# A linear-attention and gated-MLP kernel: the two x tiles move from the end of every partition to a place ahead of the weights

## The chip, the cores and the metric

The kernel runs on one core of a Trainium2 chip. The metric is the time of one execution on the device in microseconds (us); lower is better. Several executions are timed and their median is given, and one further execution is recorded by the hardware profiler; all rows below come from that one.

## The reference

A recurrence over 768 steps (batch 4, 8 heads of 48 channels) gives y, and y, laid out as 3072 tokens of 384 channels, goes through a gated two-layer network.

```python
for t in range(S):
    kt, vt, rt = (k[:, :, t], v[:, :, t], r[:, :, t])
    cur = np.einsum('bhd,bhe->bhde', u[None] * kt, vt)
    y[:, :, t] = np.einsum('bhd,bhde->bhe', rt, state + cur)
    state = w[None, :, :, None] * state + np.einsum('bhd,bhe->bhde', kt, vt)
...
x = np.ascontiguousarray(y.transpose(0, 2, 1, 3)).reshape(B * S, H * D)
gate = 1.0 / (1.0 + np.exp(-(x @ w_gate)))
val = x @ w_val
return (gate * val @ w_out).astype(np.float32)
```

The decays w are drawn between 0.85 and 0.95.

## The kernel before, in words

**Tiling.** Time is cut into 12 chunks of 64 steps; two chunks make one x tile of 512 columns (64 steps by 4 batches, twice), so there are six x tiles, `xt[0]` to `xt[5]`. Each is `[128, 4, 2, 512]` in four-byte numbers, 16,384 bytes in every partition: the second index is a group of channels, the third tells the rounded value from its rest. Products are made in three passes (rest of weights by rounded x, rounded by rounded, rounded weights by rest of x), so that they come near full precision.

**Recurrence.** For each of 24 groups (chunk, half of the heads) the kernel loads `chan` (r and k by channel) and `toks` (k and v by token), makes scores, applies them, and adds the state's part; `x_high` (L465, ScalarE) writes the rounded result from PSUM into the x tile, `x_low` (L469, VectorE) the rest, and `fills` (L473, DMA) moves the fourth group's rows into the free rows of the other three.

**Network.** For each x tile and each of 12 slices f of the hidden dimension, `up` (L506) makes two outputs with 9 matmuls of 512 columns each, one PSUM bank after the other; `sigmoid` (L515), `product` (L519), `h_high` (L524) and `h_low` (L528) make the tile `h`; `down` (L544) adds 9 matmuls to three accumulators in three banks, in turn; for the last slice of a tile, `down` goes through the accumulators one after the other instead. Weights come once from memory, are joined from two words, split into rounded value and rest, and stay in SBUF as `wx`, 12 tiles.

**Order.** The order of the instructions on every engine is fixed: a list of steps written out by hand (`START`) up to slice 11 of the first x tile, then a loop over the other five tiles, in which `SLOTS` says after which slices a group of the recurrence is done. All DMAs go through SyncE's queue.

**Places in SBUF.** Pools are laid out one behind the other in the order in which they are opened: the constants (`const`, up to byte 33,792 of each partition, with what lies ahead of it), the weights (`wp`, 33,792 to 144,384), `hp` with the tile `sg` (to 148,480), `hq` with `h` (to 156,672), `wtmp` with `wf` (to 165,888), then `ach` with three `chan` (to 178,176), `atk` with three `toks` (to 187,776), `adk` with two `dec` (to 195,968) and `xp` with the two slots of the x tiles, 195,968 to 212,352 and 212,352 to 228,736. Even x tiles lie in the first slot, odd ones in the second. In `const` lie among others `score` (from 18,112) and `state` (from 22,208).

**General path.** `ach`, `atk`, `adk` and `xp` belong to `main`, which is closed at the end (L695). Then every engine reads a flag and branches (L696, L697): only if a decay is outside 0.5 to 2 is the whole work done again by a slower path, whose tiles take the place that `main` gave up. With these inputs that path isn't entered.

Of the kernel before, what the change touches and what calls it, by code (L numbers as in the profile page):

```python
# [10 lines left out]
F32 = mybir.dt.float32  # L11
F32R = mybir.dt.float32r
# [8 lines left out]
P = 128  # L21
# [4 lines left out]
CT = B * C  # L26
# [33 lines left out]
def rwkv_then_moe(ctx: ExitStack, tc: tile.TileContext, wd, ub, ch, tk, rt, wt, rk0, vn0, wd0, out):  # L60
    nc = tc.nc

    const = ctx.enter_context(tc.tile_pool(name="const", bufs=1))
    wp = ctx.enter_context(tc.tile_pool(name="wp", bufs=1))
    hp = ctx.enter_context(tc.tile_pool(name="hp", bufs=2))
    hq = ctx.enter_context(tc.tile_pool(name="hq", bufs=2))
# [4 lines left out]
    main = ctx.enter_context(ExitStack())  # L71
    ach = main.enter_context(tc.tile_pool(name="ach", bufs=3))
    atk = main.enter_context(tc.tile_pool(name="atk", bufs=3))
    adk = main.enter_context(tc.tile_pool(name="adk", bufs=2))
    xp = main.enter_context(tc.tile_pool(name="xp", bufs=2))


    def two_banks():
# [173 lines left out]
    xt, dec, ga, yb = {}, {}, {}, {}  # L252
# [297 lines left out]
    def accumulators():  # L550
        return [pacc.tile([P, 512], F32, name=f"acc{d}") for d in range(3)]

    def store(acc, dst):
        for d in range(3):
            if d < 2:
                wide = wtmp.tile([P, W3], F32, name="wf")
            o = wide[:, 512 * (d // 2) : 512 * (d // 2) + 512]
            nc.scalar.copy(out=o[:, 0:CT], in_=acc[d][:, 0:CT])
            nc.vector.tensor_copy(o[:, CT:], acc[d][:, CT:])
            nc.sync.dma_start(  # L560
                out=out[d * P : (d + 1) * P, dst], in_=o.rearrange("q (c t) -> q c t", t=CT)
            )
# [70 lines left out]
    for step in START.split():  # L633
        name, _, arg = step.partition(".")
# [62 lines left out]
    with tc.If(bad != 0):  # L697
        with ExitStack() as g:
            gp = g.enter_context(tc.tile_pool(name="gp", bufs=1))
# [21 lines left out]
            with tc.For_i(0, NC) as c:  # L721
# [38 lines left out]
                    out=xg[bass.ds(c, 1)].rearrange("o q p t -> (o q) p t"),  # L760
                    in_=yc.rearrange("q p b i -> q p (b i)"),
                )
            xr = gp.tile([P, 3, 2, CT], F32, name="xr")
            x = gp.tile([P, 3, 2, 512], F32R, name="xgr")
            with tc.For_i(0, NC, 2) as c:
                for j in range(3):
                    for to, lo, n, p in (
                        (0, 0, D, j), (64, 64, D, j), (D, 16 * j, 16, 3), (64 + D, 64 + 16 * j, 16, 3),
                    ):
                        nc.sync.dma_start(  # L770
                            out=xr[to : to + n, j],
                            in_=xg[bass.ds(c, 2), lo : lo + n, p].rearrange("c q t -> q c t"),
                        )
                xf = xr.rearrange("q j c t -> q j (c t)")
                nc.vector.tensor_copy(x[:, :, 0], xf)
                nc.vector.tensor_tensor(x[:, :, 1], xf, x[:, :, 0], ALU.subtract)
                m = Moe(x, accumulators(), slice(0, 512))
                for f in range(NF):
                    m.up(f)
                    m.gate(f)  # L780
                    if f:
                        m.down(f - 1)
                m.down(NF - 1)
                store(m.acc, bass.ds(c, 2))
# [90 lines left out]
```

## Time and profile before

| | |
|---|---|
| median of 3 runs | 558.22 us (557.37 to 559.66) |
| the profiled execution's own time | 559.26 us |
| its span, first to last instruction | 557.5 us |
| TensorE matmuls busy | 521.9 us (94% of the span) |
| VectorE, ScalarE, GpSimd busy | 235.4, 184.1, 212.9 us |
| DMA | 47.84 MB, mean 86 GB/s |
| instructions in the profile | 11987 |

The own time is longer than the span by 1.8 us, which lie before the first and behind the last instruction. Busy times of several engines overlap; a matmul's duration reaches into the next one's, so that its pace is read from the starts of consecutive groups.

### The profile page before, as it was taken

How to read it: one execution, taken by the hardware profiler on the slowest of the kernel's cores; microseconds unless marked ns; L12 is line 12 of the kernel's file. 1: busy time of each engine (PE TensorE's matmuls, PEld its weight loads, DVE VectorE, ACT ScalarE, POOL GpSimd, SP SyncE). 2: the span in 40 equal slices, each digit the busy share in tenths (PEclk: the TensorE clock that was granted, in tenths of full speed). 3: DMA queues.
4: the chain of work that ended last, by engine and by line, in shares of the span. 5: the costliest groups of instructions: out<-in, count | busy, mean ns of one | idle time of the engine just before them, and what ended most of it. 6: DMA issues, size and time to landing. Idle time of an engine off the chain costs nothing. (4 is left out here: it accounts for less than half of the span.)

```text
span 557.5 us, 11987 instructions
## 1 busy us (share of the span) xinstructions
PE 521.9 (94%) x5204; PEld 427.1 (77%) x5204; DVE 235.4 (42%) x364; ACT 184.1 (33%) x394; POOL 212.9 (38%) x165
## 2 busy tenths in 40 slices
PE   1596899999999999999999999999999999999994
PEld 1486778777888888888888888888888888888883
DVE  7798799786524414324414324314324110101001
ACT  4466454633422322422322422322322221221111
POOL 3534234648254424254424254424234121111220
PEclk9998799999999999999999999999999999999998
DMA  8698911040221303221303221303220001100001
GB/s 329 265 364 311 368 36 54 30 111 2 88 83 52 92 16 86 79 77 67 92 15 88 77 80 65 93 13 89 78 75 5 11 1 19 58 0 1 0 1 61
DMA packets 15723, 47.84 MB, mean 86 GB/s; under 512 B 2384, under 2 KB 5200, under 8 KB 14256
## 3 DMA queue, kind: packets, MB, share of 16 engines
q1 hardware_dynamic: 15664, 47.01, 24.7%
q8 instruction: 43, 0.70, 0.5%
q14 instruction: 16, 0.13, 0.1%
HBM read 39.92 MB, written 4.72 MB: 80 GB/s over the span
## 5 line engine op out<-in xcount | busy, mean ns | idle before, releaser
L506 PE MATMUL ring<-xt,wx 128*128 128x512 f32 (+1 forms) x1332 | 317.8, 392 | 1.2 <-PE sc L366 0.8
L506 PEld LDWEIGHTS ring<-xt,wx 128*128 128x128 f32 x1332 | 248.2, 191 | 57.7 <-PE sc L366 0.9
L528 POOL TENSOR_TENSOR h<-sg,h 128x512 fp32r<-128x512 f32 x68 | 97.6, 1435 | 272.4 <-ACT h L524 272.4
L544 PE MATMUL acc<-h,wx 128*128 128x512 f32 (+1 forms) x666 | 164.6, 391 | 2.6 <-DVE h L528 1.3
L519 DVE TENSOR_TENSOR sg<-ring,sg 128x512 f32<-128x512 f32 (+1 forms) x74 | 50.0, 676 | 247.0 <-PE ring L506 247.0
L544 PEld LDWEIGHTS acc<-h,wx 128*128 128x128 f32 x666 | 122.4, 190 | 29.6 <-DVE h L528 1.5
L515 ACT ACTIVATE sg<-ring 128x512 f32<-128x512 f32 (+1 forms) x74 | 43.3, 586 | 158.9 <-PE ring L506 158.9
L524 ACT CAST h<-sg 128x512 fp32r<-128x512 f32 (+1 forms) x74 | 45.0, 608 | 150.6 <-DVE sg L519 150.6
L284 POOL TENSOR_TENSOR dec<-chan,tabk 128x512 f32<-128x512 f32 x22 | 30.7, 1397 | 12.4 <-ACT xt L465 6.9
L469 DVE TENSOR_TENSOR xt<-ring,xt 112x256 fp32r<-112x256 f32 (+1 forms) x52 | 20.0, 419 | 34.6 <-ACT xt L465 32.9
L249 POOL TENSOR_TENSOR wx<-wf,wx 128x1152 fp32r<-128x1152 f32 (+1 forms) x9 | 23.7, 2639 | 24.1 <-ACT wx L246 24.1
L295 DVE TENSOR_TENSOR chan<-chan,tabk 128x512 f32<-128x512 f32 x24 | 28.8, 1201 | 2.9 <-ACT dec L278 2.9
L366 PE MATMUL sc<-dec,chan 48*64 48x64 f32 x768 | 17.9, 236 | 12.2 <-DVE chan L295 10.2
L305 POOL TENSOR_TENSOR dec<-dec,toks 128x384 f32<-128x384 f32 x16 | 16.8, 1050 | 24.6 <-DMA dec<-in_rt 24.5
L366 PEld LDWEIGHTS sc<-dec,chan 48*64 48x64 f32 x768 | 15.3, 148 | 13.6 <-DVE chan L295 9.4
L299 POOL TENSOR_TENSOR toks<-toks,tabn 128x384 f32<-128x384 f32 x19 | 25.4, 1342 | 0.0
L374 DVE COPY_PREDICATED score<-masks,sc 128x512 f32<-128x512 int32 x32 | 23.9, 746 | 0.7
L328 PE MATMUL ring<-score,toks 64*48 64x64 f32 (+1 forms) x768 | 17.0, 226 | 7.5 <-DVE score L374 6.5
L419 ACT ACTIVATE state<-state,pw 112x96 f32<-112x96 f32 x80 | 23.4, 364 | 0.3 <-PE ring L328 0.2
L328 PEld LDWEIGHTS ring<-score,toks 64*48 64x48 f32 (+1 forms) x768 | 14.5, 134 | 8.6 <-issue 7.4
L240 DVE SCALAR_TENSOR_TENSOR wf<-wr,wf 128x1152 int32<-128x1152 int32 (+1 forms) x13 | 20.2, 1552 | 0.4
L239 DVE SCALAR_TENSOR_TENSOR wf<-wr,wf 128x1152 int32<-128x1152 int32 (+1 forms) x13 | 19.8, 1523 | 0.5
(61 smaller groups left out, 275.2 us busy)
## 6 DMA issues: line engine op xcount, KB each, us to landing
wr<-in_wt SPq DMA_DIRECT2D x11, 1152.0 KB, 11.9
chan<-in_ch SPq DMA_DIRECT2D x24, 512.0 KB, 4.0
toks<-in_tk SPq DMA_DIRECT2D x24, 400.0 KB, 4.4
out_y<-wf SPq DMA_DIRECT2D x17, 256.0 KB, 2.3
dec<-in_rt SPq DMA_DIRECT2D x16, 192.0 KB, 2.7
xt<-xt SPq DMA_DIRECT2D x30, 64.0 KB, 2.3
wr<-in_wt SPq DMA_DIRECT2D x2, 576.0 KB, 5.3
xt<-xt SPq DMA_DIRECT2D x12, 32.0 KB, 3.6
```

The costliest lines, as they stand in the source:

```text
L284: eng.tensor_tensor(v4(t[:, 0]), v4(chan[n][:, 0]), bc2(table_of(n)[:, :, ::-1]), ALU.mult)
L295: nc.vector.tensor_tensor(v4(k), v4(k), bc2(table_of(n)), ALU.mult)
L299: eng.tensor_tensor(v4(k), v4(k), bc2(tabn[:, 4 * g : 4 * g + 4]), ALU.mult)
L328: nc.tensor.matmul(yb[n][bank][64 * half : 64 * half + m, cs], lhsT, rhs, start=first, stop=stop, skip_group_check=True,)
L366: nc.tensor.matmul(sc[64 * gm : 64 * gm + 64, be, o : o + C], kk[row, cs : cs + C], rr[row, cs : cs + C], start=True, stop=True,)
L374: nc.vector.copy_predicated(t.rearrange("q (b m i) -> q b m i", b=2, m=4), masks[:, m].bitcast(I32).unsqueeze(1).unsqueeze(1).broadcast_to ...
L506: nc.tensor.matmul(o[:, self.cols], w[a][:, g * DM + kt * P : g * DM + (kt + 1) * P], self.x[:, kt, b, self.cols], start=(k == 0), stop=(k ...
L515: nc.scalar.activation(sg[:, c], self.pair[f][0][:, c], AF.Sigmoid)
L519: nc.vector.tensor_tensor(sg[:, c], self.pair.pop(f)[1][:, c], sg[:, c], ALU.mult)
L524: nc.scalar.copy(out=h[:, 0, c], in_=sg[:, c])
L528: eng.tensor_tensor(h[:, 1, c], self.sg.pop(f)[:, c], h[:, 0, c], ALU.subtract)
L544: nc.tensor.matmul(self.acc[d][:, self.cols], w[a][:, 2 * DM + d * P : 2 * DM + (d + 1) * P], h[:, b, self.cols], start=(f == 0 and k == 0 ...
```

## The change

The pool of the x tiles, `xp`, is opened right behind `const` and no longer as the last of `main`. With that the x tiles lie at bytes 33,792 to 66,560, and every pool from `wp` to `adk` lies 32,768 bytes higher: the weights at 66,560 to 177,152, `h` at 181,248 to 189,440, `wf` to 198,656, `chan` to 210,944, `toks` to 220,544, `dec` to 228,736. As `main` now gives up less room, the general path takes its two large tiles, `xr` and `x`, from `xp`.

```diff
@@ -61,6 +61,7 @@
     const = ctx.enter_context(tc.tile_pool(name="const", bufs=1))
+    xp = ctx.enter_context(tc.tile_pool(name="xp", bufs=2))
     wp = ctx.enter_context(tc.tile_pool(name="wp", bufs=1))
...
     adk = main.enter_context(tc.tile_pool(name="adk", bufs=2))
-    xp = main.enter_context(tc.tile_pool(name="xp", bufs=2))
...
-            xr = gp.tile([P, 3, 2, CT], F32, name="xr")
-            x = gp.tile([P, 3, 2, 512], F32R, name="xgr")
+            wide = xp.tile([P, 4, 2, 512], F32, name="xt")
+            xr = wide[:, 0:3, 0].rearrange("q j (c t) -> q j c t", t=CT)
+            x = xp.tile([P, 4, 2, 512], F32R, name="xt")[:, 0:3]
...
-                xf = xr.rearrange("q j c t -> q j (c t)")
+                xf = wide[:, 0:3, 0]
```

## Rows read from the trace of the kernel before

**Rows 1.** Stretches: busy us (count) of PE, PEld, DVE, ACT, POOL; clock, DMA, GB/s.

```profile
0.00:150.00 150.00, 121.70 (x1789) 102.37 (x1790) 123.17 (x163) 75.21 (x155) 71.38 (x53) 0.97 0.48 175
150.00:548.00 398.00, 398.00 (x3410) 323.49 (x3408) 111.16 (x199) 107.90 (x238) 140.98 (x112) 1.00 0.17 52
```

**Rows 2.** TensorE's longest waits, 0 to 150 us: total, times, longest.

```profile
PE sc L366 <- DVE chan L295: 10.2, 2, 9.4
PE ring L328 <- DVE score L374: 6.5, 2, 6.1
```

**Rows 3.** Timeline of TensorE, a slice of xt[4]: start, us, count.

```profile
440.20 4.36 PE L506 MATMUL ring<-xt,wx 128*128 128x512 f32 x18
444.39 2.22 PE L544 MATMUL acc<-h,wx 128*128 128x512 f32 x9
446.45 0.86 PE L506 MATMUL ring<-xt,wx 128*128 128x512 f32 x3
```

**Rows 4.** Timeline of TensorE, a slice of xt[5].

```profile
491.45 4.35 PE L506 MATMUL ring<-xt,wx 128*128 128x512 f32 x18
495.64 2.22 PE L544 MATMUL acc<-h,wx 128*128 128x512 f32 x9
497.70 4.36 PE L506 MATMUL ring<-xt,wx 128*128 128x512 f32 x18
```

**Rows 5.** Timeline of TensorE, a slice of xt[1].

```profile
210.29 4.34 PE L506 MATMUL ring<-xt,wx 128*128 128x512 f32 x18
214.47 2.25 PE L544 MATMUL acc<-h,wx 128*128 128x512 f32 x9
216.56 4.35 PE L506 MATMUL ring<-xt,wx 128*128 128x512 f32 x18
```

**Rows 6.** The last down: matmuls running at 549.2 and 550.5 us; its weight loads.

```profile
548.99 0.39 PE L544 MATMUL acc<-h,wx 128*128 128x512 f32 x1
...
550.15 0.39 PE L544 MATMUL acc<-h,wx 128*128 128x512 f32 x1
...
548.65 1.46 PEld L544 LDWEIGHTS acc<-h,wx 128*128 128x128 f32 x7 [0.78 <-POOLq L697]
```

**Rows 7.** Groups of the whole span: count, busy us, mean ns, idle before.

```profile
L519 DVE TENSOR_TENSOR sg<-ring,sg 128x256 f32<-128x256 f32 x4 | 1.7, 419 | 3.0 <-PE ring L506 3.0
L469 DVE TENSOR_TENSOR xt<-ring,xt 112x256 fp32r<-112x256 f32 x44 | 16.6, 419 | 32.3 <-ACT xt L465 32.3
L465 ACT CAST xt<-ring 112x256 fp32r<-112x256 f32 x44 | 13.8, 364 | 6.4 <-PE ring L328 6.4
L558 ACT COPY wf<-acc 128x256 f32<-128x256 f32 x15 | 5.5, 373 | 2.5 <-PE acc L544 2.4
```

**Rows 8.** Groups from 150 to 548 us: small matmuls and weight loads.

```profile
L328 PE MATMUL ring<-dec,state 48*64 48x64 f32 x240 | 10.2, 224 | 0.0
L328 PE MATMUL ring<-score,toks 64*64 64x64 f32 x240 | 9.5, 218 | 0.0
L328 PEld LDWEIGHTS ring<-score,toks 64*64 64x64 f32 x240 | 8.2, 135 | 0.0
L328 PEld LDWEIGHTS ring<-dec,state 48*64 48x64 f32 x240 | 8.2, 134 | 5.6 <-issue 5.6
```

**Rows 9.** GpSimd's groups from 150 to 548 us.

```profile
L528 POOL TENSOR_TENSOR h<-sg,h 128x512 fp32r<-128x512 f32 x59 | 80.9, 1372 | 234.2 <-ACT h L524 234.2
L284 POOL TENSOR_TENSOR dec<-chan,tabk 128x512 f32<-128x512 f32 x13 | 16.9, 1302 | 0.0
```

**Rows 10.** GpSimd's groups on chan and toks, 0 to 150 us.

```profile
L284 POOL TENSOR_TENSOR dec<-chan,tabk 128x512 f32<-128x512 f32 x9 | 13.8, 1534 | 12.4 <-ACT xt L465 6.9 <-ACT wx L246 5.6
L299 POOL TENSOR_TENSOR toks<-toks,tabn 128x384 f32<-128x384 f32 x7 | 9.6, 1376 | 0.0
```

**Rows 11.** The branch at the end: count, ns min/median/max, start us.

```profile
L697 ACTq COMPARE_BRANCH  x1: 50/50/50, 551.3 to 551.3; - x1
L697 SPq COMPARE_BRANCH  x1: 45/45/45, 553.1 to 553.1; - x1
```

## The prediction

> **What bounds the kernel now.** I read the busy times by stretch first [rows 1]. From 150 to 548 us TensorE is busy for 398.00 of 398.00 us at a granted clock of 1.00 (the 2.4 GHz level), while GpSimd is busy for 140.98, VectorE for 111.16 and ScalarE for 107.90 us: nothing but the pace of the matmuls sets the time there. From 0 to 150 us TensorE is busy for 121.70, so it idles for 28.3 us; there VectorE is the busiest of the others, with 123.17 us. Then TensorE's waits of that first stretch [rows 2]: 10.2 us for the scaled keys in `chan` and 6.5 us for the masked `score` make 16.7 of the 28.3, the recurrence's preparation by VectorE. From 548 us to the end of the span at 557.5 lie 9.5 us in which the last matmuls, the stores and the closing waits run.
>
> So a change of place can act in three ways: on the pace of matmuls while TensorE is full, on the vector engines' instructions while TensorE waits for them, and on the branch at the end.
>
> To get the pace I took the timeline of TensorE and looked at starts of groups, since a matmul's own 0.39 us reach into the next. In a slice of `xt[4]` [rows 3] the 18 matmuls of `up` take 444.39 - 440.20 = 4.19 us, 232.8 ns each, and the 9 of `down` 446.45 - 444.39 = 2.06 us, 228.9 ns each. In a slice of `xt[5]` [rows 4] it is again 4.19 and 2.06. The even tile lies at byte 195,968 and the odd one at 212,352, and the two slices use different weight tiles (f = 7 and f = 3), yet the pace is equal to the hundredth of a microsecond.
>
> **The change part by part.**
>
> *Instructions.* On every engine the order is written by hand and the diff touches none of it up to the branch: no instruction, DMA or wait is added, removed or moved past another in SyncE's queue or any other. The only edits of code besides the pool's place are inside the branch, which isn't entered. What moves is places: x down by 162,176 bytes, everything from the weights to `dec` up by 32,768. Both shifts are multiples of 128 bytes, so no tile's start changes relative to a boundary of 4 to 128 bytes. Cost of this part: 0.
>
> *Matmuls that read x.* 70 full slices of 18 matmuls, 1260, read x from its new place while they load weights from theirs. The trace has no 512-column read from below byte 66,560. The nearest rows are the small ones [rows 8]: as moving operand `score` (byte 18,112 on) costs a mean of 218 ns and `dec` (187,776 on) 224 ns; as weights `state` (22,208 on) loads in 134 ns and `toks` (178,176 on) in 135. So the low end of a partition costs nothing over the high end, and the weights, moved within what these rows span, nothing either. The pace in [rows 3, 4] says the same for weights of one slice and another. I take 0.
>
> What would a gain be? `down` is 3.9 ns quicker per matmul than `up`, and it reads `h` from the middle (148,480 on). If the whole difference were the price of reading x at the end, 1260 x 3.9 ns = 4.9 us would come back. But the two also differ in the order of outputs: `up` adds 9 times to one bank, `down` goes around three. The last `down` tells these apart [rows 6]: there `h` is read while one accumulator is finished after the other. Its weight loads are 7; the matmul that starts at 548.99 is the second and the one at 550.15 the seventh, so five steps take 1.16 us, 232 ns each: `up`'s pace, with `h` as operand. The 3.9 ns go with the order of outputs and not with the place of x. I keep -4.9 us as the lower bound.
>
> The Trainium skill, on its page "TensorE: Matmul & The Clock Gate", section "Wait — 56ns, not 53.3ns?", gives 215.7 ns from start to start for 512 columns at the full clock, measured there in bf16; no row here is as quick, and if all of `up`'s excess of 17.1 ns over that page's figure came from the place of x and vanished, an estimate by that page would be 1260 x 17.1 ns = 21.5 us less. The trace disagrees with that reading, since a `down` that reads no x is above the figure too.
>
> An upper bound comes from a slice of `xt[1]` [rows 5], where TensorE ran in a slightly slower rhythm: 216.56 - 210.29 = 6.27 us for the 27 matmuls, against 6.25 in the others. If other places led all 58 slices between 150 and 548 us into it, that is 58 x 0.02 = +1.2 us. There is no reason for it in the rows; I take 0.
>
> *Writers of x.* ScalarE's write into x and VectorE's read and write of it, at the end of the partition, cost 364 and 419 ns [rows 7]; the same engines' instructions of nearly the same size on `wf` and `sg` in the middle cost 373 and 419. No dependence on place again, and after 150 us these have TensorE's full queue as cover. Cost 0. The copies among x's own rows are the same transfers in the same queue.
>
> *What takes x's place.* `chan`, `toks` and `dec` now lie above byte 195,968, with the end of `wf`. For VectorE, ScalarE, DMA and TensorE's moving reads the rows on x just given cover that end. GpSimd has no row there. Its nearest are an instruction on `sg` and `h` (144,384 to 156,672), 1372 ns, and one of the same size on `chan`, `tabk` and `dec` (up to byte 195,968), 1302 ns [rows 9]: no rise with place, 70 ns between two places in the middle. Before 150 us GpSimd runs 16 instructions on `chan` and `toks`, 23.4 us [rows 10]; 16 x 70 ns is 1.1 us either way, if each delayed TensorE in full. Later GpSimd is idle for 398.00 - 140.98 = 257.0 us, which hides it. I take 0.
>
> *General path.* Taking tiles from `xp` can make its first users wait for the last readers of x. If such a wait stood ahead of the branch, it would be met: ScalarE branches at 551.3 and SyncE at 553.1 us [rows 11], and the last `down`, which follows every `up` on TensorE, is under way at 548.99 [rows 6]. Cost 0; without that cover, at most the length of the wait on SyncE, which does nothing after it but wait for the stores.
>
> *Sum.* Against the profiled execution: 559.26 (span 557.5 and 1.8 around it) + 0 = 559.26 us. The median of the runs is 1.04 us lower, 558.22, so I forecast 558.2. With the bounds: -4.9 - 1.1 = -6.0, that is 552.2, and +1.2 + 1.1 = +2.3, that is 560.5.
>
> **The rivals.**
>
> *Faster: x is slow to read at the end.* Then `up` falls to `down`'s pace and the time to 558.2 - 4.9 = 553.3 us. For it: `up` is slower than `down` in every slice, and x is the operand that differs. Against it: the last `down` [rows 6]. Chance 0.11.
>
> *Slower: the end is slow for GpSimd.* `chan`, `toks` and `dec` are what GpSimd works on while TensorE waits in the first 150 us. The place is its two groups there, 23.4 us [rows 10]; they lengthen the start by over 0.5% (2.8 us) once each instruction takes 12% more and all of it reaches TensorE. At 25%, 5.9 us come on top: 564.1 us. For it: no row has GpSimd at that end. Against it: no engine whose rows reach that end pays for it, and TensorE's long waits there are for VectorE [rows 2]. Chance 0.09.
>
> *Something else changes with the places.* The general path's borrowed tiles put a wait ahead of the branch; it ends under the cover given above and the time stays 558.2. I count it with the forecast.
>
> **How the numbers follow.** About 0.5% (2.8 us) is what a measurement of this kernel can tell from no change; the three runs before span 0.4%. No change within 555.4 to 561.0: 0.80. Faster: 0.11, slower: 0.09. The likeliest time is 558.2, with a range of its own from 555.4 to 561.0. The range that I give starts at the sum's lower bound, 552.2, which takes in the faster rival, and ends at 561.0, which takes in the upper bound of 560.5; it leaves out the slower rival and little else.
>
> **What the profile after would show.** If each step is right: the same 11987 instructions; a span within 2 us of 557.5; `up` in 4.19 and `down` in 2.06 us per slice in tiles of both slots; L465 near 364 and L469 near 419 ns; L284 near 1302 ns between 150 and 548 us; TensorE idle for about 28 us before 150 us, for the same releasers. The prediction is wrong if `up`'s 4.19 changes by 0.05 us or more (70 slices make 3.5 us of it), or if the idle time of the start changes by 3 us, which would point to the vector engines' or the loads' places, or to a wait that I don't see in the text.

## The result and the profile after

The changed kernel takes 550.78 us (median of 4 runs, 549.82 to 551.15) against 557.86 for the kernel before (4 runs, 557.37 to 559.66). The estimated ratio is 0.9865, with a 95% interval of 0.9838 to 0.9891. It is faster by 7.1 us in the medians, where no change was forecast. The profiled execution took 549.82 us with a span of 548.0; before it was 559.26 and 557.5.

The timeline of TensorE in the kernel after, one slice of `xt[4]` and one of `xt[5]`, answers to [rows 3, 4]:

```profile
439.35 4.24 PE L506 MATMUL ring<-xt,wx 128*128 128x512 f32 x18
443.43 2.20 PE L544 MATMUL acc<-h,wx 128*128 128x512 f32 x9
445.47 0.84 PE L506 MATMUL ring<-xt,wx 128*128 128x512 f32 x3
...
489.62 4.24 PE L506 MATMUL ring<-xt,wx 128*128 128x512 f32 x18
493.69 2.20 PE L544 MATMUL acc<-h,wx 128*128 128x512 f32 x9
495.74 0.62 PE L506 MATMUL ring<-xt,wx 128*128 128x512 f32 x2
```

`up` now takes 443.43 - 439.35 = 4.08 us instead of 4.19, 226.7 ns per matmul instead of 232.8, and `down` 2.04 instead of 2.06, 226.7 ns as well. Both go at one pace. A slice takes 6.12 us instead of 6.25. The fall of 0.11 us in `up` is over twice the 0.05 that the prediction had named as a sign of being wrong.

That `down` had this pace already in the kernel before, and lost it only at its start, is seen in the slice of [rows 3], from the start of its fourth matmul:

```profile
445.09 0.39 PE L544 MATMUL acc<-h,wx 128*128 128x512 f32 x1
```

The first three matmuls, right behind `up`, take 445.09 - 444.39 = 0.70 us, 233 ns each; the other six take 446.45 - 445.09 = 1.36 us, 226.7 ns each. The 228.9 ns of the prediction is the mean of the two.

The pace of these groups is where the time went. From the first `up` of `xt[1]` to the last group of `down` the timelines give 545.62 - 138.69 = 406.93 us before and 536.53 - 136.77 = 399.76 after: 7.2 of the 9.5 us between the two spans. Of the rest, 1.9 us lie ahead of `xt[1]` and 0.4 at the end. Ten full slices of `xt[0]` at 0.13 us make 1.3 of the 1.9; what made the other 0.6 was not traced (the mean granted clock up to 150 us was 0.98 after and 0.97 before, so it need not be the places).

What was forecast to stay did stay. First the stretch to 150 us (columns as in [rows 1]), then groups of the whole span, two of which answer to [rows 7], and GpSimd's on `dec` between 150 and 541 us ([rows 9]):

```profile
0.00:150.00 150.00, 122.21 (x1798) 103.77 (x1799) 123.60 (x164) 75.25 (x155) 71.94 (x53) 0.98 0.48 180
...
L469 DVE TENSOR_TENSOR xt<-ring,xt 112x256 fp32r<-112x256 f32 x44 | 16.6, 418 | 33.2 <-ACT xt L465 33.2
L465 ACT CAST xt<-ring 112x256 fp32r<-112x256 f32 x44 | 13.8, 363 | 8.3 <-PE ring L328 8.3
L506 PE MATMUL ring<-xt,wx 128*128 128x512 f32 x1260 | 297.3, 389 | 0.0
...
L284 POOL TENSOR_TENSOR dec<-chan,tabk 128x512 f32<-128x512 f32 x13 | 16.7, 1288 | 0.0
```

The writers of x keep 418 and 363 ns, GpSimd's work on `chan` and `dec`, now at the end of the partition, 1288 ns; TensorE idles for 150 - 122.21 = 27.8 us at the start. What changed is the matmuls of 512 columns that read x: 297.3 us busy, where the page before had 305.0.

The last `down` of the kernel after, as in [rows 6]:

```profile
539.91 0.40 PE L544 MATMUL acc<-h,wx 128*128 128x512 f32 x1
...
541.06 0.39 PE L544 MATMUL acc<-h,wx 128*128 128x512 f32 x1
...
539.57 1.46 PEld L544 LDWEIGHTS acc<-h,wx 128*128 128x128 f32 x7 [0.80 <-POOLq L697]
```

Five steps still take 541.06 - 539.91 = 1.15 us, 230 ns each, although the slices above go at 226.7. So this group is slow where x has no part in it, and where both operands are as in the fast slices. It follows a wait of TensorE, for the last `h`. A wait isn't needed for it: a `down` of `xt[1]` that follows small matmuls does the same. Its second and seventh matmul, and the groups behind it:

```profile
205.39 0.39 PE L544 MATMUL acc<-h,wx 128*128 128x512 f32 x1
...
206.55 0.39 PE L544 MATMUL acc<-h,wx 128*128 128x512 f32 x1
...
207.23 4.24 PE L506 MATMUL ring<-xt,wx 128*128 128x512 f32 x18
211.31 2.20 PE L544 MATMUL acc<-h,wx 128*128 128x512 f32 x9
213.35 0.84 PE L506 MATMUL ring<-xt,wx 128*128 128x512 f32 x3
```

Five steps take 206.55 - 205.39 = 1.16 us, 232 ns each; the last three matmuls of the same group take 0.68 us, 226.7 ns each. So in both groups the first matmuls behind a break are slow though their operands agree, and a group's pace has to be read from its later ones.

### The profile page after: what moved, and what is told of

The parts are those of the page before. It is cut to its first block, busy times and chain, and to the rows that moved or that the text cites. A ratio compares the mean times of both kernels' runs of the same rounds, so it can differ in the third digit from the quotient of the medians.

```text
span 548.0 us, 11987 instructions
## 1 busy us (share of the span) xinstructions
PE 513.3 (94%) x5204; PEld 426.8 (78%) x5204; DVE 234.7 (43%) x364; ACT 183.9 (34%) x394; POOL 212.3 (39%) x165
## 5 line engine op out<-in xcount | busy, mean ns | idle before, releaser
L506 PE MATMUL ring<-xt,wx 128*128 128x512 f32 (+1 forms) x1332 | 310.5, 387 | 1.5 <-issue 1.4
L544 PE MATMUL acc<-h,wx 128*128 128x512 f32 (+1 forms) x666 | 162.7, 388 | 2.5 <-POOL h L528 1.2
L295 DVE TENSOR_TENSOR chan<-chan,tabk 128x512 f32<-128x512 f32 x24 | 27.1, 1128 | 2.9 <-ACT dec L278 2.9
L240 DVE SCALAR_TENSOR_TENSOR wf<-wr,wf 128x1152 int32<-128x1152 int32 (+1 forms) x13 | 20.2, 1552 | 0.5
L465 ACT CAST xt<-ring 112x256 fp32r<-112x256 f32 (+1 forms) x52 | 16.7, 363 | 10.5 <-PE ring L328 9.4
```

The lines of the kernel that those rows point to most:

```text
L295: nc.vector.tensor_tensor(v4(k), v4(k), bc2(table_of(n)), ALU.mult)
L506: nc.tensor.matmul(o[:, self.cols], w[a][:, g * DM + kt * P : g * DM + (kt + 1) * P], self.x[:, kt, b, self.cols], start=(k == 0), stop=(k ...
L544: nc.tensor.matmul(self.acc[d][:, self.cols], w[a][:, 2 * DM + d * P : 2 * DM + (d + 1) * P], h[:, b, self.cols], start=(f == 0 and k == 0 ...
```

## The experiments

x had moved in two ways: to another place, and to another remainder. Before, its slots started at 195,968 and 212,352 bytes, 384 past a multiple of 1024; the weights and `h` start at multiples of 1024 in both kernels, and so does x after the change. Four theories: **place** (the upper end is slow for the streamed operand), **order** (x has to lie ahead of the weights), **start address** (x has to start at a multiple of some power of two) and, from w_128 on, **relative place** (x and the weights have to start at the same remainder). The kernels differ in pools alone. `pad384` stands for a pool that keeps 384 bytes free. Each ratio is an estimate against executions of the kernel before that were timed beside the run; their medians were 557.5 to 558.7 us.

**late_0: x nearly at the end, but at a multiple of 1024.**

```diff
     ach = main.enter_context(tc.tile_pool(name="ach", bufs=3))
+    xp = main.enter_context(tc.tile_pool(name="xp", bufs=2))
     atk = main.enter_context(tc.tile_pool(name="atk", bufs=3))
     adk = main.enter_context(tc.tile_pool(name="adk", bufs=2))
-    xp = main.enter_context(tc.tile_pool(name="xp", bufs=2))
```

> The layout of before with one move: the x pool stands between chan and toks, so the two x tiles start at bytes 178,176 and 194,560, both multiples of 1024 (before: 195,968 and 212,352, both 384 past one); weights and h stay where they were. The second slot covers nearly the bytes of the first slot of before. Theory start address (the pace hangs on the remainder of x's first byte, not on the place): up takes 4.08 us per slice in all tiles, time 550 to 552 us. Theory place (the upper end of a partition is slow to read for the matmul): tiles of the second slot stay at 4.19 us, those of the first fall to 4.08, time near 554.5. Theory order (x has to lie ahead of the weights): 4.19 in all tiles, 558 us.

550.09 us, ratio 0.9832 (0.9801 to 0.9862). The timeline in `xt[5]`, whose slot covers nearly the bytes of the first slot of before:

```profile
482.80 4.24 PE L506 MATMUL ring<-xt,wx 128*128 128x512 f32 x18
486.88 2.20 PE L544 MATMUL acc<-h,wx 128*128 128x512 f32 x9
488.92 4.24 PE L506 MATMUL ring<-xt,wx 128*128 128x512 f32 x18
```

4.08 and 2.04 us. Place and order fall: x lies behind the weights and near the end, and the whole gain is there.

**mid_384: x in the middle, with the remainder of before.** `pad384` and `xp` stand between `wtmp` and `ach`.

> The layout of before with the x pool behind wf in the middle of the partition, and 384 bytes left free ahead of it: x at 166,272 and 182,656, 384 past a multiple of 1024 as before. Weights and h as before. Theory start address: 4.19 us per slice of up in all tiles, 557 to 559 us. Theory place: 4.08, about 551 us. Theory order: 4.19, 558 us.

557.77 us, ratio 0.9981 (0.9958 to 1.0004): no change from before.

```profile
482.89 4.35 PE L507 MATMUL ring<-xt,wx 128*128 128x512 f32 x18
487.08 2.22 PE L545 MATMUL acc<-h,wx 128*128 128x512 f32 x9
489.13 4.36 PE L507 MATMUL ring<-xt,wx 128*128 128x512 f32 x18
```

**low_384: the changed kernel, with x moved by 384 bytes.**

```diff
+    ctx.enter_context(tc.tile_pool(name="pad384", bufs=1)).tile([P, 96], F32, name="pad384")
     xp = ctx.enter_context(tc.tile_pool(name="xp", bufs=2))
+    ctx.enter_context(tc.tile_pool(name="pad128", bufs=1)).tile([P, 32], F32, name="pad128")
```

> The changed kernel with 384 bytes left free ahead of x and 128 behind it: x at 34,176 and 50,560 (384 past a multiple of 1024), weights, h and the rest 512 bytes higher, multiples of 512. Theory start address: up back at 4.19 us per slice, 557 to 559 us although x lies ahead of the weights. Theories place and order: 4.08 us, 550 to 552 us. If down slows too, its operands need more than a multiple of 512.

559.34 us, ratio 1.0004 (0.9982 to 1.0026).

```profile
484.15 4.36 PE L508 MATMUL ring<-xt,wx 128*128 128x512 f32 x18
488.35 2.22 PE L546 MATMUL acc<-h,wx 128*128 128x512 f32 x9
490.40 4.36 PE L508 MATMUL ring<-xt,wx 128*128 128x512 f32 x18
```

`up` is back at 4.20 us. All of the change is in here, x ahead of the weights and the general path with its tiles from `xp`, and nothing of its gain; so neither of these two is worth anything measurable.

**end_128: before, with 128 bytes left free ahead of x.**

```diff
+    main.enter_context(tc.tile_pool(name="pad128", bufs=1)).tile([P, 32], F32, name="pad128")
     xp = main.enter_context(tc.tile_pool(name="xp", bufs=2))
```

> The layout of before with 128 bytes left free ahead of x at the end: x at 196,096 and 212,480, multiples of 512 but not of 1024. Theory start address: 4.08 us per slice and 550 to 552 us if a multiple of 512 is enough, 4.19 and 558 if it has to be 1024. Theories place and order: 4.19 us, 558 us.

550.13 us, ratio 0.9827 (0.9793 to 0.9861). The slice below takes 4.07 us and 2.05. One line does what the change did, without moving a pool past another, and a multiple of 512 is enough.

```profile
484.99 4.24 PE L507 MATMUL ring<-xt,wx 128*128 128x512 f32 x18
489.06 2.20 PE L545 MATMUL acc<-h,wx 128*128 128x512 f32 x9
491.11 4.24 PE L507 MATMUL ring<-xt,wx 128*128 128x512 f32 x18
```

**two_256_64 and two_128_32: how small a remainder still costs.** x in the middle, a pool for each slot, so that even and odd tiles of one run have different remainders. The edit is that of two_256_64; two_128_32 keeps 128 and 416 bytes free in place of 256 and 320.

```diff
+    main.enter_context(tc.tile_pool(name="pad256", bufs=1)).tile([P, 64], F32, name="pad256")
+    xpa = main.enter_context(tc.tile_pool(name="xpa", bufs=1))
+    main.enter_context(tc.tile_pool(name="pad320", bufs=1)).tile([P, 80], F32, name="pad320")
+    xpb = main.enter_context(tc.tile_pool(name="xpb", bufs=1))
...
-            xt[ti] = xp.tile([P, 4, 2, 512], F32R, name="xt")
+            xt[ti] = (xpa, xpb)[ti % 2].tile([P, 4, 2, 512], F32R, name="xt")
```

> x in the middle of the partition, a pool for each slot: even tiles at 166,144 (256 past a multiple of 512), odd tiles at 182,848 (64 past one). How small a remainder still costs: if the start has to be a multiple of 512, up takes 4.19 us per slice in all tiles. If 256 is enough, even tiles take 4.08 and odd ones 4.19. If 64 is enough, 4.08 in all and 551 us.

> The same with even tiles at 166,016 (128 past a multiple of 512) and odd tiles at 182,816 (32 past one). If a multiple of 512 or of 256 is needed, up takes 4.19 us per slice in all tiles; if the cost grows with the remainder, odd tiles lie between 4.08 and 4.19.

In the first, a slice of `xt[4]` (remainder 256 of 512), one of `xt[5]` (64) and one of `xt[1]` (64 too):

```profile
437.74 4.24 PE L509 MATMUL ring<-xt,wx 128*128 128x512 f32 x18
441.82 2.20 PE L547 MATMUL acc<-h,wx 128*128 128x512 f32 x9
443.86 4.24 PE L509 MATMUL ring<-xt,wx 128*128 128x512 f32 x18
...
506.90 4.28 PE L509 MATMUL ring<-xt,wx 128*128 128x512 f32 x18
511.02 2.25 PE L547 MATMUL acc<-h,wx 128*128 128x512 f32 x9
513.11 4.28 PE L509 MATMUL ring<-xt,wx 128*128 128x512 f32 x18
...
167.94 4.36 PE L509 MATMUL ring<-xt,wx 128*128 128x512 f32 x18
172.14 2.24 PE L547 MATMUL acc<-h,wx 128*128 128x512 f32 x9
174.22 2.01 PE L509 MATMUL ring<-xt,wx 128*128 128x512 f32 x8
```

A remainder of 256 is free (4.08 and 2.04 us); one of 64 costs, but not always in the same way: 4.12 and 2.09 us in `xt[5]`, 4.20 and 2.08 in this slice of `xt[1]`. The 4.19 expected for `up` was met in some slices only, and part of the cost stands in `down`, whose operands agree. In the second run both remainders cost: 4.19 and 2.05 us with 128 in `xt[4]`, 4.20 and 2.06 with 32 in `xt[5]`. Each run was timed once, at 555.03 and 559.49 us, so the slices and not these times carry the reading. What counts is the remainder of 256, and among 32, 64 and 128 the cost of a slice differs little (6.21 to 6.28 us against 6.12).

**w_128 and all_384: whose start?** In the first, x and `h` start at multiples of 512 and the weights 128 bytes past one; in the second everything, x, weights and `h`, starts 384 past one.

```diff
+    ctx.enter_context(tc.tile_pool(name="pad128", bufs=1)).tile([P, 32], F32, name="pad128")
     wp = ctx.enter_context(tc.tile_pool(name="wp", bufs=1))
+    ctx.enter_context(tc.tile_pool(name="pad384", bufs=1)).tile([P, 96], F32, name="pad384")
```

(w_128, on top of late_0; all_384 is low_384 without its second pad.)

> x between chan and toks at 178,688 and 195,072 and h at 148,992, all multiples of 512; the weights start 128 bytes past one (33,920). Theory moving operand (only the start of the operand that streams counts): up stays at 4.08 and down at 2.04 us per slice, 550 to 552 us. Theory relative place (x and the weights must start at the same remainder): up at 4.19 and down slower than 2.06, 558 us or more. If weight loads have a rule of their own, their mean leaves 188 ns.

> The changed kernel with 384 bytes left free ahead of x: x at 34,176, weights at 66,944, h at 181,632, all 384 past a multiple of 512. Theory relative place: up 4.08 and down 2.04 us per slice, 550 to 552 us. Theory moving operand: up at 4.19 as before, and down slows as well since h has lost its multiple of 512, by 9 x 6 ns to about 2.10 us; 58 slices make some 4 us more than before, 561 to 563 us.

w_128: 560.93 us, ratio 1.0050 (1.0027 to 1.0073), slower than before, with x and `h` both at multiples of 512:

```profile
440.94 4.35 PE L508 MATMUL ring<-xt,wx 128*128 128x512 f32 x18
445.13 2.25 PE L546 MATMUL acc<-h,wx 128*128 128x512 f32 x9
447.22 4.34 PE L508 MATMUL ring<-xt,wx 128*128 128x512 f32 x18
```

all_384: 551.01 us, ratio 0.9883 (0.9861 to 0.9905), with neither x nor `h` at a multiple of 512:

```profile
484.44 4.24 PE L507 MATMUL ring<-xt,wx 128*128 128x512 f32 x18
488.52 2.20 PE L545 MATMUL acc<-h,wx 128*128 128x512 f32 x9
490.56 4.24 PE L507 MATMUL ring<-xt,wx 128*128 128x512 f32 x18
```

The theory that all runs so far had left standing, that x's own start address decides, falls twice over: an aligned x is slow (4.19 us) beside weights that are 128 off, and an x that is 384 off is fast (4.08) beside weights that are off by as much. It is the relation of the two. (The mean duration of a weight load, for which w_128's expectation had a theory, stayed at 188 ns.)

**x_w_128 and h_384: the relation, each half by itself.** x_w_128 is before with the two pads of w_128: x stays last, with its remainder of before (128 of 256), the weights get the same, and `h` now differs from them. h_384 is late_0 with `pad384` ahead of `hq` and `pad128` behind it: only `h` differs.

> The layout of before, x still last in every partition (196,480 and 212,864) with its remainder of before (128 past a multiple of 256), but the weights moved to the same remainder (33,920), and h at 148,992, a multiple of 256. Theory relative place (the streamed operand and the weights have to start at the same remainder of 256): up falls to 4.08 us per slice though x keeps place and remainder, and down, whose h now differs from the weights, slows from 2.06 to about 2.09; 58 slices give -0.108 + 0.03 us each, 553 to 555 us. Theory place or theory start address of x alone: up stays at 4.19, 558 us or more.

> x between chan and toks and the weights at multiples of 512, h alone at 148,864, 128 past a multiple of 256. Theory relative place: down slows to about 2.09 us per slice (as in the run with the weights 128 off), up stays near 4.08 but for its first matmuls; 58 slices make 3 to 4 us on top of 550.1, 553 to 554.5 us. If only x's matmuls can be slowed, because their 18 go to one bank nine times in a row, down stays at 2.04 and the time at 550 us.

x_w_128: 554.06 us, ratio 0.9926 (0.9897 to 0.9956).

```profile
487.18 4.27 PE L508 MATMUL ring<-xt,wx 128*128 128x512 f32 x18
491.28 2.26 PE L546 MATMUL acc<-h,wx 128*128 128x512 f32 x9
493.38 4.27 PE L508 MATMUL ring<-xt,wx 128*128 128x512 f32 x18
```

h_384: 555.55 us, ratio 0.9947 (0.9926 to 0.9969).

```profile
443.63 4.27 PE L508 MATMUL ring<-xt,wx 128*128 128x512 f32 x18
447.73 2.26 PE L546 MATMUL acc<-h,wx 128*128 128x512 f32 x9
449.83 2.45 PE L508 MATMUL ring<-xt,wx 128*128 128x512 f32 x10
```

Both times `up` takes 4.10 us and `down` 2.10, 233 ns per matmul: with `h` as with x, a streamed operand whose start differs from the weights' is slow. h_384 took some 1 us more than the 553 to 554.5 expected; 0.02 us in each of 58 `up`s make that much. `up`'s last 0.02 us are a remnant of the `down` ahead of it, as `down`'s 2.06 instead of 2.04 was of `up` in the kernel before.

## Why the prediction was wrong

**What failed: "Both shifts are multiples of 128 bytes, so no tile's start changes relative to a boundary of 4 to 128 bytes. Cost of this part: 0".** The arithmetic was right and stopped one power of two too early, and with it the term *Matmuls that read x*, put at 0, was wrong. x moved by 162,176 bytes down and the weights by 32,768 up; relative to the weights x went from a remainder of 128 to 0 of 256 bytes, and that made 1260 matmuls quicker by 232.8 - 226.7 = 6.1 ns. 1260 x 6.1 is 7.7 us, as is the fall of the group's busy time from 305.0 to 297.3. The runs on either side of this remainder (late_0, end_128, all_384 fast; mid_384, low_384, w_128 slow) show it. The rows that were to price the move, [rows 8], could not: 218 and 224 ns are mean durations of small matmuls and not their pace, and their weights are slices of `toks` and `state` that start 192 bytes apart, so that many remainders are mixed in each mean.

**What hid it: the reading of the last `down` [rows 6].** It was to tell the order of outputs from the place of the operand, and its 232 ns were taken as `up`'s pace. But after the change the same group still took 230 ns per step while `up` and `down` both went at 226.7. It follows a wait, and its first matmuls are slow as those at 205.39 are; the comparison stood on the one `down` that is not in the steady rhythm. The 3.9 ns between `up` and `down` had been x's, as the faster rival assumed, and so had the 2.2 ns more that `down` lost behind `up`.

**The faster rival** had the right sign and instructions (chance 0.11, 553.3 us) with a wrong mechanism: late_0 and mid_384 show that the upper end is not slow. Its size was too small, 4.9 us, since it let `up` fall to `down`'s mean of 228.9 ns, and the first three matmuls of `down` were held up by the `up` ahead of it; both fell to 226.7. The lower bound of 552.2 rested on the same 228.9. The trace of before had the right pace in it, in `down`'s last six matmuls.

**The equal pace of slices in [rows 3, 4]** was read as a sign that place doesn't matter. It was none: 12 weight tiles of 9,216 bytes and two slots of 16,384 are 36 and 64 times 256 bytes apart, so every slice had the same remainder.

**What held.** The instructions are the same 11987. The writers of x (418 and 363 ns), GpSimd at the end of the partition (1288 ns) and the idle time at the start (27.8 us) stayed; the slower rival did not come. The general path's borrowed tiles cost nothing (low_384). The other rhythm of [rows 5] went too; the slice of `xt[1]` that answers to it, shown above from 207.23 to 213.35, takes 4.08 and 2.04 us in the kernel after.

The Trainium skill, on its page "TensorE: Matmul & The Clock Gate", section "Step-by-step: what each phase is for", says that loading the next weights takes no read bandwidth from the running matmul. No run here measured a read bandwidth or took the loads away, so none shows whether that holds; what they show is that a matmul of 512 columns takes some 6 ns more (232.8 against 226.7) where its two starts differ by 128 bytes. The 215.7 ns from start to start that the Trainium skill gives on the same page, section "Wait — 56ns, not 53.3ns?", was reached by none of the kernels, and 226.7 was the steady pace of each of the fast ones.

**What stays open** is why. That the weight load, which runs beside the matmul of the weights before it, meets the streamed operand's reads in time would fit the dependence on both starts, but no run took the load away, and the mean duration of a load from 150 to 541 us is 188 ns in w_128 as in the kernel after, so this is argued and not shown. No differences but 32, 64, 128 and 256 bytes were tried, nor whether other types or column counts have the same rule. No version measured is faster than late_0 and end_128, which the changed kernel equals within its spread.

## What to carry to other kernels

Where TensorE is full, work out the start address of every operand in a partition, and compare the streamed operand with the weights, by the remainder of 256 bytes: a pool of odd size (three `toks` of 3,200 bytes here) ahead of an operand can cost 2.6% of the time of its matmuls, and a pad of 128 bytes gives it back here. Read the pace of matmuls from starts in steady groups that follow neither a wait nor small matmuls, from the later ones of a group, for every operand pair; two groups of the same shape at different paces are a question to be settled by a run, and not by one untypical group. When a layout changes, look at differences between operands, and not only at each tile's own shift.

## What the runs showed that I had not expected

The pace of 512-column matmuls depends on two start addresses together: 226.7 ns when they agree in the remainder of 256 bytes, some 232 to 233 ns when they differ by 32 or 128, and between 229 and 233 when they differ by 64. The slower rhythm outlasts its cause: in x_w_128 `up`, whose operands agree, takes 4.10 us behind a slow `down` and 4.08 behind a fast one (all_384), and in `xt[5]` of two_256_64 `down`, whose operands agree, takes 2.09 us behind `up` at a difference of 64. Whether small matmuls have the rule isn't shown. In mid_384 `toks` moved by 33,152 bytes, 128 past a multiple of 256, and `score` didn't, and their matmuls of 64 columns kept the mean of 218 ns of [rows 8]; but that mean mixes many remainders in either kernel, and it is a duration and not a pace.
